# First weight pieces rounded and fetched later, and three more pairs turned by 32 x 32 squares

## The chip, the cores and the metric

The kernel runs on one core of a Trainium2 chip. The metric is device time in microseconds (us) of that core. The time before is the median of three runs, 1395.97 us (1393.84 to 1398.77).

## The reference

Attention with RMS-normalised q and k, 8 batches of 12 heads, 448 tokens, 64 dimensions; then two matrix products with `h - tanh(h)` between them on the 3584 x 768 result.

```python
q_n, k_n = rmsnorm(q, g_q), rmsnorm(k, g_k)          # x / sqrt(mean(x*x) + 1e-6) * g
scores = scale * matmul(q_n, k_n.transpose(0, 1, 3, 2))
scores = scores - max(scores)                        # over the last axis
attn = exp(scores)
attn = attn / (sum(attn) + 1e-9)
out = matmul(attn, v)                                # (8, 12, 448, 64)
x = out.transpose(0, 2, 1, 3).reshape(3584, 768)
h = x @ w_in                                         # 768 x 2048
g = h - tanh(h)
return g @ w_out                                     # 2048 x 768
```

w_in and w_out come as float64. The kernel takes them as pairs of 32-bit words and rounds them to float32 on the chip.

## The kernel before

**Pairs and slots.** The unit of attention is a pair of heads: 8 batches of six pairs (`NP`) are 48 pairs, counted from 0, so the 16th pair is pair 15. The program is a list of slots written out by hand; slot s finishes pair s, makes the scores of pair s+1, turns (transposes) q and k of pair s+2 and squares or normalises pair s+3. Slots -3 to 5 are `first_slot` (L943), 6 to 11 `early_slot` (L977), 12 to 47 `slot` (L1005). Instructions go to each engine's queue in the order in which this code makes them: PE (matmuls), ACT (exps, copies, squares), DVE, POOL, and SP, which issues nearly all DMAs.

**The MLP.** While attention of batch b+1 runs, a generator gives the matmuls of batch b's two products; `run(ns)` puts that many ns of them between the parts of a slot. In `first_slot` there is no MLP work yet. Later batches read their weights from a ring of six places in `w_f`, fetched five products ahead (`ring_load`, L379).

**Weights.** There are 32 pieces (`PIECES`) of 768 KB raw, 16 of w_in and 16 of w_out. `weight_load(n)` (L254) fetches one, as four DMAs for w_in. The first eight (`EARLY`) land in the memory that is `gT` later, which has four places (`NSTAGE`); the others in three buffers `w_raw`. Rounding has three steps: `round_weight_a` (two ACT instructions, L71 and L72), `round_weight_b` (three on DVE, L78 to L82) and `round_weight_c` (one on POOL, L90). `weight(to)` (L290) rounds up to `to` pieces: step a of piece n, steps b and c of piece n-1, and then it fetches on to piece n+3, as long as a place is free (`place_free`). The last lines of `first_slot(s)` call it with `8 * (s + 3) // 8`, that is one piece by the end of slot -2 and one more in each slot after. Piece 0 is fetched before all slots.

**q and k, two ways.** The plain way: `load` fetches q of a pair so that each of 112 partitions holds four neighbouring tokens, and k in blocks of 128; `squares` (ACT) and `norm` (DVE, POOL) give each token's factor, `norm_q` scales q, and `turn` (L416) transposes k and q with eight PE matmuls against the identity (L421, L425) and two ACT copies. k's factor goes into the exp as its scale (`rr`). The way by blocks: `load_blocks` (L439) fetches squares of 32 tokens by 32 dimensions in eight DMAs, `square_blocks` (ACT), `norm_blocks` (DVE and one POOL power), `scale_blocks` (DVE), and `turn_blocks` (two DVE transposes, one ACT scaling): no PE instruction. The exp then needs no scale. The tiles of this way live in a pool that is opened when the first batch's MLP has been written out (`late["blocks"]`), after slot 11.

Which way a pair goes, and in which order tokens lie, is set by one constant: `FIRST, NJ = 3, S // BL` (L434) and

```python
def by_blocks(s):
    return has(s) and steps[s][0] >= FIRST
```

so pairs from 18 on (batch 3) go by blocks. `store` (L822), which transposes and writes the result, undoes the plain way's order of tokens for batches below `FIRST`.

## Time and profile before

| what | us |
|---|---|
| median of three runs | 1395.97 |
| lowest, highest | 1393.84, 1398.77 |
| profiled execution, device time | 1397.86 |
| its span, first to last instruction | 1396.1 |
| DVE, ACT, POOL busy | 940.3, 507.9, 555.4 |
| DMA engines busy (queue of SP), share | 63.8% |
| q_nat loads, issue to landing, median | 4.5 |
| gT loads (weight pieces), issue to landing, median | 4.2 |
| qk_nat loads (blocks), issue to landing, median | 2.3 |

In the lines below, a timeline row gives start, duration, engine, line, operation, `output<-input`, shapes and how often, and in brackets how long the engine sat idle before it and what ended that. `SPq` rows are DMAs being issued. PE's matmul ends are modelled, so that a busy PE need not be PE at its peak. Each fp32 matmul counts twice in some rows of the timeline.

### The profile page before, as it was taken

What the parts mean: (1) busy time and instruction counts of PE and PEld (TensorE: products, weight loads), DVE (VectorE), ACT (ScalarE), POOL (GpSimd) and SP (SyncE); (2) the same over time, 40 slices, a digit from 0 to 9 for tenths busy, and PEclk for the clock granted to TensorE, in tenths of its full rate; (3) what the DMA queues carried; (4) which work ended last, traced back from release to release, by engine and by line L of the source; (5) the groups of instructions that cost most, each with busy time, mean ns of one, the idle gap of its engine ahead of it and who ended that gap; (6) DMA issues with size and microseconds to landing.
All of it is one profiled execution on the core that took longest, in us unless ns stands there. A gap on an engine that the chain in (4) does not pass through costs nothing.

```text
span 1396.1 us, 29929 instructions
## 1 busy us (share of the span) xinstructions
PE 1360.6 (97%) x11864; PEld 1133.3 (81%) x11864; DVE 940.3 (67%) x1530; ACT 507.9 (36%) x1153; POOL 555.4 (40%) x348
## 2 busy tenths in 40 slices
PE   6999899999999999999999999999999999999997
PEld 2468664478899898889889988988988998899997
DVE  3999888757756688567867668656885677632311
ACT  5866554234423433233332333224333243301100
POOL 4665555224432347224544245423462255402310
PEclk9999999999999999999999999999999999999999
DMA  7769788765556756666656666666556656366663
GB/s 177 175 189 245 244 253 214 207 198 166 158 142 192 182 163 182 170 155 193 181 148 176 195 156 184 184 156 176 171 166 176 172 179 192 100 189 183 192 192 89
DMA packets 355273, 250.01 MB, mean 179 GB/s; under 512 B 266484, under 2 KB 297396, under 8 KB 355124
## 3 DMA queue, kind: packets, MB, share of 16 engines
q1 hardware_dynamic: 355120, 248.00, 63.8%
q8 instruction: 96, 1.57, 0.5%
q14 instruction: 53, 0.43, 0.1%
q10 hardware_dynamic: 4, 0.00, 0.0%
HBM read 214.50 MB, written 33.42 MB: 178 GB/s over the span
## 4 chain that ended last, share of the span: by engine, by line
PE 87%; DVE 5%; DMA 3%; ACT 2%; SPq 1%; issue 1%; POOL 0%; DVEq 0%; ACTq 0%
PE mm L733 65%; PE sc L506 9%; PE sc L567 6%; PE mm L898 4%; PE sc L555 1%; DMA q_nat<-in_q_dram 1%; PE sc L605 1%; DMA w_raw<-in_moe_w_out_dram 1%; DMA w_f<-w_out 1%; DMA w_raw<-in_moe_w_in_dram 1%; DVE w_out L82 1%; PE mm L605 1%; DVE w_out L78 0%; DVE rs L631 0%; ACT p L512 0%
## 5 line engine op out<-in xcount | busy, mean ns | idle before, releaser
L733 PE MATMUL mm<-xT,w_f 128*128 128x224 f32 x1392 | 278.2, 354 | 1.4 <-DVE s L789 1.4
L733 PEld LDWEIGHTS mm<-xT,w_f 128*128 128x128 f32 x1392 | 261.3, 190 | 15.0 <-issue 10.2
L733 PEld LDWEIGHTS mm<-gT,w_f 128*128 128x128 f32 x1344 | 252.8, 190 | 12.8 <-issue 12.8
L733 PE MATMUL mm<-gT,w_f 128*128 128x224 f32 x1344 | 263.0, 354 | 0.0
L506 PE MATMUL sc<-qT,kT 64*32 64x448 f32 (+1 forms) x3072 | 219.1, 505 | 12.8 <-ACT p_last L512 9.4
L463 POOL TENSOR_TENSOR rr_mine<-rr_mine,neg_half 128x28 f32<-128x28 f32 x30 | 145.1, 4835 | 203.3 <-DVE rr_mine L462 203.3
L733 PE MATMUL mm<-tt,w_f 128*128 128x224 f32 x1044 | 208.7, 353 | 0.0
L733 PEld LDWEIGHTS mm<-tt,w_f 128*128 128x128 f32 x1044 | 197.0, 190 | 4.4 <-issue 4.4
L733 PE MATMUL mm<-tg,w_f 128*128 128x224 f32 x1008 | 197.7, 353 | 0.0
L770 POOL TENSOR_TENSOR gT<-s,th 128x448 f32<-128x448 f32 x96 | 118.6, 1245 | 188.1 <-ACT th L769 181.6
L733 PEld LDWEIGHTS mm<-tg,w_f 128*128 128x128 f32 x1008 | 190.6, 190 | 0.0
L506 PEld LDWEIGHTS sc<-qT,kT 64*32 64x32 f32 x3072 | 72.3, 107 | 84.3 <-issue 58.8
L671 DVE TENSOR_TENSOR xT<-xT,sc 128x448 f32<-128x448 f32 x35 | 21.7, 621 | 163.3 <-PE sc L506 118.5
L693 POOL TENSOR_TENSOR tt<-xT,tt 128x224 f32<-128x224 f32 x23 | 31.4, 1366 | 240.5 <-DVE xT L675 217.5
L650 ACT COPY sum_g<-sum 32x14 f32<-32x14 f32 x280 | 56.2, 201 | 180.8 <-DVE sum L642 175.0
L567 PE MATMUL sc<-p,v_nat 64*32 64x448 f32 x1120 | 110.5, 536 | 0.0
L769 ACT ACTIVATE th<-s 128x448 f32<-128x448 f32 x96 | 55.3, 576 | 114.4 <-DVE s L795 57.2
L135 POOL TENSOR_TENSOR rr<-rr,neg_half 112x8 f32<-112x8 f32 (+1 forms) x36 | 59.6, 1676 | 61.5 <-DVE rr L134 37.4
L512 ACT ACTIVATE p<-sc 128x448 f32<-128x448 f32 x120 | 65.2, 543 | 46.8 <-PE sc L506 34.5
L898 PE MATMUL mm<-gT,w_out 128*128 128x448 f32 x192 | 76.8, 556 | 0.3 <-POOL w_out L90 0.3
L898 PEld LDWEIGHTS mm<-gT,w_out 128*128 128x128 f32 x192 | 36.6, 195 | 39.3 <-issue 37.2
L567 PEld LDWEIGHTS sc<-p,v_nat 64*32 64x32 f32 x1120 | 40.6, 107 | 31.1 <-issue 31.1
(151 smaller groups left out, 1853.1 us busy)
## 6 DMA issues: line engine op xcount, KB each, us to landing
w_f<-w_in SPq DMA_DIRECT2D x196, 384.0 KB, 3.3
w_f<-w_out SPq DMA_DIRECT2D x147, 512.0 KB, 3.8
w_raw<-in_moe_w_out_dram SPq DMA_DIRECT2D x16, 768.0 KB, 5.0
out_dram<-th SPq DMA_DIRECT2D x192, 56.0 KB, 1.9
w_in<-w_out SPq DMA_DIRECT2D x21, 384.0 KB, 6.7
qk_nat<-in_q_dram SPq DMA_DIRECT2D x120, 56.0 KB, 2.3
qk_nat<-in_k_dram SPq DMA_DIRECT2D x120, 56.0 KB, 2.4
gT<-in_moe_w_in_dram SPq DMA_DIRECT2D x32, 192.0 KB, 4.2
```

The source lines that it names most:

```text
L135: nc.gpsimd.tensor_tensor(out=r, in0=r, in1=neg_half[:rows], op=ALU.pow)
L463: nc.gpsimd.tensor_tensor(out=mine, in0=mine, in1=neg_half[:, :1].to_broadcast([P, 2 * NJ]), op=ALU.pow)
L506: nc.tensor.matmul(tiles[h][i * BL : (i + 1) * BL, :n], lhsT=kT[r, c * P + at : c * P + at + BL], rhs=qT[r, first : first + n], start=True ...
L512: nc.scalar.activation(p[:, h, c if c < 2 else 0, :], tiles[h][:, :n], AF.Exp, scale=1.0 if rr is None else rr[:, 0, 2 * c + h : 2 * c + h ...
L567: nc.tensor.matmul(av[g][i * BL : (i + 1) * BL, :S], lhsT=v_nat[keys, h, c, m * BL : (m + 1) * BL], rhs=p[keys, h], start=first, stop=True ...
L605: nc.tensor.matmul(av[n][r : r + BL, :HS], lhsT=v_nat[:, h, c, m * BL : (m + 1) * BL], rhs=p[c][:, h, n * HS : (n + 1) * HS], start=False, ...
L650: nc.scalar.copy(out=acc[h * BL : (h + 1) * BL, g], in_=part[g * BL : (g + 1) * BL, h * NJ : (h + 1) * NJ])
L693: eng.tensor_tensor(out=t2, in0=x22, in1=t1, op=ALU.subtract)
L733: nc.tensor.matmul(bank[:, f * HS : (f + 1) * HS], lhsT=w[:, c * width + f, :], rhs=moving[p](c), start=(first and f == 0 and c == 0), sto ...
L769: nc.scalar.activation(th, h, AF.Tanh, bias=0.0, scale=1.0)
L770: eng.tensor_tensor(out=g[:, rows, cols], in0=h, in1=th, op=ALU.subtract)
L898: nc.tensor.matmul(bank[:, :S], lhsT=w_out_row(f, n // HC)[:, n % HC * P : (n % HC + 1) * P], rhs=g[:, f, :], start=(f == 0), stop=(f == C ...
```

## The change

1. `weight` no longer fetches itself but calls a new `load_weights(to)`; for pieces below 5 it fetches on to piece n+2 in place of n+3. At the end of slot -2, nothing is rounded: `load_weights(2)` fetches piece 1 alone. Piece 0 is rounded at the end of slot -1, together with piece 1.
2. `FIRST` goes from 3 to 2, and now sets the order of tokens alone (`in_order`): pairs from 12 on are fetched with rows in natural order, with new branches in `fetch` for q and k (q in two DMAs for one, all in pieces of 256 bytes). `store` takes plain columns from batch 2 on.
3. `by_blocks` asks for `s >= TURNED`, 2 * 6 + 3 = 15. Pairs 15, 16 and 17 go by blocks too. Pair 15's blocks are fetched near the end of slot 12; the others as before at the start of a slot.

On the engines' queues: PE loses 24 transposes; ACT has piece 0's two instructions 14 places later; on SP, the twelve weight DMAs of slot -2 become four and the four of slot -1 become eight; the fetching stays one piece behind the old order until slot 3, where the two are level again.

```diff
@@ fetch
     if name == "q":
+        if in_order:
+            for h in range(2):
+                nc.sync.dma_start(out=t[:, h], in_=pair[h].rearrange("(c p) d -> p c d", c=NCH))
+            return
...
     if name == "v":
         last = t[:, :, KF]
+    elif in_order:
+        last = t[:, KF]
     if in_order:
         for h in range(2):
-            nc.sync.dma_start(out=t[:, h, :KF], in_=pair[h, : KF * P].rearrange("(c p) d -> p c d", p=P))
+            to = t[:, h, :KF] if name == "v" else t[:, :KF, h]
+            nc.sync.dma_start(out=to, in_=pair[h, : KF * P].rearrange("(c p) d -> p c d", p=P))
@@ load
-                fetch(nc, name, t, src[b, 2 * hp : 2 * hp + 2], by_blocks(s))
+                fetch(nc, name, t, src[b, 2 * hp : 2 * hp + 2], in_order(s))
@@ weight
+    def load_weights(to):
+        while done[0] < min(to, PIECES) and place_free(done[0]):
+            weight_load(done[0])
+            done[0] += 1
...
-            while done[0] < min(n + 4, PIECES) and place_free(done[0]):
-                weight_load(done[0])
-                done[0] += 1
+            load_weights(n + (3 if n < EARLY - 3 else 4))
@@ order of tokens, blocks
-    FIRST, NJ = 3, S // BL
+    FIRST, NJ = 2, S // BL
+    TURNED = 2 * NP + 3
     def by_blocks(s):
+        return has(s) and s >= TURNED
+    def in_order(s):
         return has(s) and steps[s][0] >= FIRST
@@ first_slot
-        weight(EARLY * (s + 3) // (NP + 2))
+        if s == -2:
+            load_weights(2)
+        else:
+            weight(EARLY * (s + 3) // (NP + 2))
@@ early_slot
-        if has(s + 4):
+        if has(s + 4) and not by_blocks(s + 4):
             load(s + 4, "qk")
@@ slot
-        if by_blocks(s + 3):
+        if by_blocks(s + 3) and s + 3 > TURNED:
             load_blocks(s + 3)
...
+        if s + 3 == TURNED:
+            load_blocks(s + 3)
         if ahead:
             norm_q(s + 3)
```

## The prediction

> **What bounds the kernel now.** I read, in this order: the engines' busy shares, the chain of work that ended last, the timeline of the first 40 us, a table by stretches of the same time, and the times at which each slot's `p_last` exps start. All times are of the profiled execution: 1397.86 us, of which the span is 1396.1.

> ```profile
> PE 1360.6 (97%) x11864; PEld 1133.3 (81%) x11864; DVE 940.3 (67%) x1530; ACT 507.9 (36%) x1153; POOL 555.4 (40%) x348
> ...
> PE 87%; DVE 5%; DMA 3%; ACT 2%; SPq 1%; issue 1%; POOL 0%; DVEq 0%; ACTq 0%
> ```

> TensorE is the bound, and 87% of the last chain is its own work. So a saving is either PE work taken out, or one of the few places where PE is not last. The first 36 us are such a place:

> ```profile
> 10.00 3.24 PE L506 MATMUL sc<-qT,kT 64*32 64x448 f32 x32 [0.62 <-ACT qT L429]
> ...
> 15.19 0.89 ACT L71 ACTIVATE w_out<-gT 128x768 f32<-128x768 f32 x1 [3.98 <-DMA gT<-in_moe_w_in_dram]
> ...
> 16.11 6.39 SPq L265 DMA_DIRECT2D gT<-in_moe_w_in_dram  x12
> 16.75 2.19 ACT L512 ACTIVATE p<-sc,rr 128x448 f32<-128x448 f32 x4
> ...
> 23.25 0.31 SPq L99 DMA_DIRECT2D q_nat<-in_q_dram  x1
> ...
> 24.11 2.24 ACT L512 ACTIVATE p<-sc,rr 128x448 f32<-128x448 f32 x4
> ...
> 31.42 0.63 ACT L123 ACTIVATE n<-q_nat 112x512 f32<-112x512 f32 x1 [4.12 <-DMA q_nat<-in_q_dram]
> ...
> 36.05 2.21 ACT L512 ACTIVATE p<-sc,rr 128x448 f32<-128x448 f32 x4
> ```

> Pair 0's scores are done by 13.2, but ACT first waits 3.98 us for the first weight piece (L71) and starts the exps (L512) at 16.75. Then twelve weight DMAs (three pieces) go out in one block, the q load of pair 3 gets onto the queue only at 23.25, and ACT waits 4.12 us for it. Slot 0 therefore lasts from 24.11 to 36.05, 11.94 us; the next three, exp to exp, last 9.67, 9.51 and 9.47. Stretch by stretch, the columns being us, PE, PEld, DVE, ACT, POOL, PE clock, DMA share, GB/s:

> ```profile
> 10.00:17.00 7.00, 4.95 (x40) 2.10 (x40) 2.31 (x5) 2.91 (x5) 3.24 (x2) 1.00 0.92 219
> 17.00:24.00 7.00, 6.41 (x69) 1.97 (x70) 2.53 (x6) 7.00 (x14) 2.58 (x2) 0.76 0.98 217
> 24.00:36.00 12.00, 10.32 (x169) 4.86 (x170) 5.62 (x10) 7.71 (x15) 5.69 (x4) 1.00 0.90 199
> ```

> The transfers are saturated here (0.92 to 0.98 busy, about 217 GB/s), so the order on SP decides who waits. In the second part of the change the reader is to look at the slots' lengths:

> ```profile
> 319.51 0.79 ACT L512 ACTIVATE p_last<-sc,rr 128x224 f32<-128x224 f32 x2 [3.09 <-PE sc L506]
> ...
> 402.49 0.79 ACT L512 ACTIVATE p_last<-sc,rr 128x224 f32<-128x224 f32 x2 [8.45 <-PE sc L506]
> ...
> 429.30 0.60 ACT L512 ACTIVATE p_last<-sc 128x224 f32<-128x224 f32 x2 [5.03 <-PE sc L506]
> ...
> 456.11 0.61 ACT L512 ACTIVATE p_last<-sc 128x224 f32<-128x224 f32 x2 [5.02 <-PE sc L506]
> ```

> Slots 13, 14 and 15 take 82.98 us together; the slots after them, where q and k go by squares of 32, take 26.81 each.

> [...] exps with finished scores stand 3.98 us behind a rounding that waits for its data. [...] the trace has 0.76 in the stretch 17 to 24, after a PE wait of 2.5 us[...]. [...] a median packet of 1024 B takes 47 ns, 768 B 36, 256 B 18 and 128 B 13, that is 22, 21, 14 and 10 bytes per ns.

> **The change part by part.**

> *First weights.* Slot -2 no longer rounds piece 0 (L71, L72); both piece 0 and piece 1 are rounded at the end of slot -1, behind pair 0's exps. ACT in slot -1, from rows of the trace: chunk 0's scores are half of the 3.24 us, so ready at 11.6, and chunk 1's at 13.2; its exps end at 14.3; kT and qT of pair 1 (0.53 each) follow the transposes and end at 15.5; the squares of pair 2 wait for k, whose last piece lands at 16.8, and end at 17.4; `p_last` 0.7 and `p_full` 1.06 end at 19.2. Rounding piece 0 costs 1.65 (0.8 each), to 20.8. Rounding piece 1 must wait: its last DMA, whose place on SP is unchanged (issued at 17.69), lands at 22.2. It ends at 23.8, and slot 0's exps start then, 0.3 earlier than 24.11. So the wait at L71 is mostly turned into one for piece 1. The larger gain is in slot 0. Pieces 2 and 3 (eight DMAs, 0.86 us each on the saturated engines, 6.9 us) now stand behind pair 3's q and k, which land at about 24.4 instead of 31.3 and are wanted at 27. The 4.12 us wait is gone. What is late next is PE: the `p_last` scores get their banks at 25.0, last values and values take 3.0 to 3.6, the last scores start at 28.6 and let `p_full` start 1.1 later (as at 41.93 and 43.06), 29.7; plus 1.06 and 1.65 this gives slot 1's exps at 32.4 against 36.05: 3.65 earlier. If slot 0 takes the 9.5 of later slots instead, 33.3, or 2.75 earlier. I take 3.5, ends 2.5 and 4.2.

> Does the lag starve the rounding? Piece 2 lands after pair 3 and v of pair 1 at about 28.9, and is wanted at 30.8; piece 3 at 32.4, wanted at 40. From slot 3 (n = 5) the loads stand where they stood. DVE's and POOL's steps b and c keep their slots. From 36 us on nothing depends on absolute time: loads are released by buffers, roundings by due times counted in matmuls, so I expect the whole rest to shift by what slot 1 gained. The DMA engines are idle for 0.3 of 36 to 46 and 0.2 of 46 to 58, so the same bytes in 3.5 us less are carried.

> *Squares of 32 for pairs 15, 16, 17.* Out of PE: 3 turns of four k and four q transposes. The chain prices a turn at 0.44 + 0.39 = 0.83 us, so 2.5 us; the slots say 82.98 - 3 × 26.81 = 2.55. I take 2.5, ends 2.0 and 2.7, because the later slots already run with all the work that is added here. That is, per pair: on DVE one reduction 1.06, four copies 0.17, two small ones 0.37, the scaling 1.24, two transposes 1.27, together 4.6 us, for 2 × 0.68 + 2 × 0.17 + one `norm_q` of 0.6 to 2.7; on POOL one power of 4.78 for two of 1.62; on ACT 0.95 + 0.67 for 2.3 or so. DVE is busy 14 to 23 us in these slots of 27 to 28, POOL 10 to 12: PE hides it. Were that cover gone, the late kT would hold the next slot's first scores by the overrun alone. Pair 15's load goes from slot 11 to the end of slot 12, and its squaring from slot 12 to slot 13, some 13 us after the issue, with 2.3 us to landing: covered. SP gets eight DMAs (4.2 us) ahead of ring loads that are fetched five products ahead, each product 12 or more matmuls of 0.19 us: covered, as in all later slots.

> *Loads in order.* q and k of pairs 12 to 14 and v of pairs 12 to 17 go in pieces of 256 B: q 896 packets of 18 ns for 224 of 47, k's main part 768 of 18 for 256 of 36, over 16 engines 0.65 us more per pair, and one more issue of 0.6 us each on SP. They fall in slots 8 to 10, a slot ahead of use: nothing, at most 1.5 us if they hold up w_out pieces for which PE already waits there. Batch 2's stores read plain columns instead of strided ones: nothing.

> Sum: 3.5 + 2.5 = 6.0, so 1397.86 becomes 1391.9. The profiled execution lies 1.89 above the median of the three runs (1395.97, from 1393.84 to 1398.77); the same saving from the median gives 1390.0. A difference of 0.3%, 4.2 us, is about what a measurement of this kernel can tell from no change.

> **The rivals.** (B) *The start's gain is swallowed.* From 60 to 160 us DVE is 97% busy with roundings and combinations; if that stretch is paced by weights and not by when attention arrives, only 2.5 us remain: 1393.5. Against it: DVE is idle 1.9 of the 12 us from 46 to 58, so it carries no backlog into it, and the pieces come in by released buffers. (C) *Rounding starves.* ACT rounds in front of the next slot's exps; if piece 2 lands after 30.8 (my slack is 1.9 us) and the shorter lead keeps pieces 2 to 6 late, each by one piece's transfer of 3.45 us, five slots lose 17 us: 1407, slower. For it: transfers are saturated to 40 us. Against: one piece less is in flight than before. (D) *A later stall goes too.* At 170.91 PE waits 5.39 us for an exp behind a w_out piece, then runs the next stretch at clock 0.74; the changed phase may take away 6 us: 1384. The same phase could as well cost that; I count this in the range of the others.

> **How the numbers follow.** Forecast 0.60 at 1390.0 (its own range 1387.5 to 1392.5), B 0.22, C 0.09, D 0.09. The range 1385.5 to 1396.5 holds forecast and B whole with the unknown costs, leaving out C and D. Faster by over 0.3% means below 1391.8: 0.85 of the forecast and D, 0.60. Slower is C, 0.09. The rest, 0.31, is within 0.3%.

> **What would show it.** Right: the first exps at about 11.6; L123 of slot 0 no longer waiting for DMA; slot 1's exps near 32.4; slots 13 to 15 at 26.8 and 24 matmuls fewer on PE. Wrong: ACT waiting for `gT` in slots 0 to 3 (C); the first batch's MLP starting 3.5 us earlier but its end not (B); a new PE wait of microseconds between 160 and 290.

## The result, and the profile after

| | before | after |
|---|---|---|
| median of 20 runs, us | 1397.32 | 1393.93 |
| lowest, highest | 1393.37, 1399.12 | 1390.53, 1396.42 |
| profiled execution, its span | 1397.86, 1396.1 | 1394.93, 1393.0 |

The ratio is 0.9974, 95% interval 0.9968 to 0.9981: 3.6 us saved (interval 2.7 to 4.5) where 6.0 were forecast. The whole interval lies below 1, so the gain is real, though 3.6 us is less than the 0.3% (4.2 us) that one measurement of this kernel can tell from none. The forecast of 1390.0 lies 3.9 below the measured median: 2.6 of it because less was saved (3.4 between the medians), 1.35 because the kernel before took 1397.32 in these 20 runs and not the 1395.97 of the first three. L71 and the lines up to 90 keep their numbers; L512 became L527 (exps), L506 L521 (scores), L123 L130 (squares of q), L733 L748 (MLP), L789 L804 (a sum of the MLP on DVE).

The page of the changed kernel, busy time and the engines' shares of the chain that ended last:

```profile
PE 1358.7 (98%) x11840; PEld 1131.3 (81%) x11840; DVE 938.9 (67%) x1545; ACT 504.3 (36%) x1147; POOL 561.3 (40%) x345
...
PE 87%; DMA 4%; DVE 4%; ACT 1%; SPq 1%; issue 1%; POOL 0%; DVEq 0%; ACTq 0%
```

24 matmuls have gone (11864 to 11840), and PE still carries 87% of the chain. The timeline of ACT and PE in slot 0, after:

```profile
23.19 0.90 ACT L71 ACTIVATE w_out<-gT 128x768 f32<-128x768 f32 x1 [2.12 <-DMA gT<-in_moe_w_in_dram]
...
24.77 2.18 ACT L527 ACTIVATE p<-sc,rr 128x448 f32<-128x448 f32 x4
25.43 0.94 PE L521 MATMUL sc<-qT,kT 64*32 64x224 f32 x9 [2.82 <-ACT p L527]
27.76 0.66 ACT L130 ACTIVATE n<-q_nat 112x512 f32<-112x512 f32 x1
28.42 1.72 PE L620 MATMUL mm<-p,v_nat 128*32 128x224 f32 x16
...
33.06 3.04 PE L521 MATMUL sc<-qT,kT 64*32 64x448 f32 x48
34.43 1.16 ACT L527 ACTIVATE p_full<-sc,rr 128x448 f32<-128x448 f32 x2 [4.82 <-PE sc L521]
...
37.10 2.22 ACT L527 ACTIVATE p<-sc,rr 128x448 f32<-128x448 f32 x4
```

The wait of 4.12 us for q is gone: L130 at 27.76 has no bracket. But the last line, slot 1's exps, stands at 37.10, where before had 36.05: the start is later, not earlier. The lines are to be read from the last one upwards. The exps of `p_full` waited 4.82 us for their scores, which PE began at 33.06. In front of those on PE are the values (L620), of which a group of 16 took 1.72 us. Before them PE had waited 2.82 us for the exps, and these stood behind a rounding that waited 2.12 us for piece 1. The table by stretches, after (us, PE, PEld, DVE, ACT, POOL, PE clock, DMA share, GB/s), says why the values were slow:

```profile
17.00:24.00 7.00, 4.53 (x70) 2.24 (x70) 4.32 (x8) 4.82 (x9) 5.03 (x3) 1.00 0.98 216
24.00:36.00 12.00, 10.04 (x128) 3.86 (x128) 6.54 (x13) 7.18 (x15) 3.63 (x3) 0.72 0.94 209
```

Before, the low clock (0.76) lay in the stretch 17 to 24, where ACT was about to wait for q anyway. Now it lies in 24 to 36 (0.72), on the path. The trace's clock records give it as half speed for 6.8 us from 26.7. In the second part, the slots' `p_last` exps, first before (slots 14 and 15) and then after (slots 13 to 16):

```profile
347.16 0.79 ACT L512 ACTIVATE p_last<-sc,rr 128x224 f32<-128x224 f32 x2 [1.50 <-PE sc L506]
...
374.89 0.78 ACT L512 ACTIVATE p_last<-sc,rr 128x224 f32<-128x224 f32 x2 [1.64 <-PE sc L506]
```

```profile
318.42 0.79 ACT L527 ACTIVATE p_last<-sc,rr 128x224 f32<-128x224 f32 x2 [3.09 <-PE sc L521]
...
345.23 0.61 ACT L527 ACTIVATE p_last<-sc 128x224 f32<-128x224 f32 x2 [1.50 <-PE sc L521]
...
372.93 0.61 ACT L527 ACTIVATE p_last<-sc 128x224 f32<-128x224 f32 x2 [0.74 <-PE sc L521]
399.72 0.61 ACT L527 ACTIVATE p_last<-sc 128x224 f32<-128x224 f32 x2 [4.87 <-PE sc L521]
```

Slot 13 takes 26.81 and slot 15 26.79, but slot 14 takes 27.70, as long as before (27.73) although its turn is gone. The three save 82.98 - 81.30 = 1.68 us.

The 3.1 us of span between the two executions are thus made up: 0.1 lost by slot 7's exps (121.72 to 121.83), 1.2 gained from there to slot 12's `p_last` (290.93 to 289.84), 1.68 in slots 13 to 15, 0.3 after slot 18. The 1.2 is hardly the change's: the clock records have a half-clock stretch of 6.8 us at 240.0 before and one of 3.4 us at 241.8 after, and half of the difference, an estimate of what it cost, is 1.7.

### The profile page after: what moved, and what is told of

The parts are those of the page before. It is cut to its first block, busy times and chain, and to the rows that moved or that the text cites. A ratio compares the mean times of both kernels' runs of the same rounds, so it can differ in the third digit from the quotient of the medians.

```text
span 1393.0 us, 29913 instructions
## 1 busy us (share of the span) xinstructions
PE 1358.7 (98%) x11840; PEld 1131.3 (81%) x11840; DVE 938.9 (67%) x1545; ACT 504.3 (36%) x1147; POOL 561.3 (40%) x345
## 4 chain that ended last, share of the span: by engine, by line
PE 87%; DMA 4%; DVE 4%; ACT 1%; SPq 1%; issue 1%; POOL 0%; DVEq 0%; ACTq 0%
PE mm L748 66%; PE sc L521 8%; PE sc L582 6%; PE mm L913 4%; PE sc L570 1%; DMA w_f<-w_out 1%; DMA gT<-in_moe_w_in_dram 1%; PE sc L620 1%; DMA q_nat<-in_q_dram 1%; DMA w_raw<-in_moe_w_out_dram 1%; PE sc L641 1%; SPq L125 1%; DMA k_nat<-in_k_dram 0%; PE mm L620 0%; ACT p L527 0%
## 5 line engine op out<-in xcount | busy, mean ns | idle before, releaser
L748 PE MATMUL mm<-xT,w_f 128*128 128x224 f32 x1392 | 278.5, 355 | 1.7 <-DVE s L804 1.7
L748 PEld LDWEIGHTS mm<-xT,w_f 128*128 128x128 f32 x1392 | 261.3, 190 | 16.0 <-issue 10.2
L748 PEld LDWEIGHTS mm<-gT,w_f 128*128 128x128 f32 x1344 | 252.8, 191 | 12.8 <-issue 12.8
L748 PE MATMUL mm<-gT,w_f 128*128 128x224 f32 x1344 | 263.0, 354 | 0.0
L478 POOL TENSOR_TENSOR rr_mine<-rr_mine,neg_half 128x28 f32<-128x28 f32 x33 | 159.7, 4840 | 218.2 <-DVE rr_mine L477 218.2
L521 PE MATMUL sc<-qT,kT 64*32 64x448 f32 (+1 forms) x3072 | 216.4, 501 | 12.1 <-ACT p_last L527 8.3
L748 PE MATMUL mm<-tt,w_f 128*128 128x224 f32 x1044 | 208.8, 353 | 0.0
L748 PEld LDWEIGHTS mm<-tt,w_f 128*128 128x128 f32 x1044 | 197.0, 191 | 4.4 <-issue 4.4
L748 PE MATMUL mm<-tg,w_f 128*128 128x224 f32 x1008 | 197.5, 353 | 0.0
L748 PEld LDWEIGHTS mm<-tg,w_f 128*128 128x128 f32 x1008 | 190.7, 191 | 0.0
L521 PEld LDWEIGHTS sc<-qT,kT 64*32 64x32 f32 x3072 | 72.2, 107 | 82.3 <-issue 59.6
L527 ACT ACTIVATE p<-sc 128x448 f32<-128x448 f32 x132 | 71.7, 543 | 51.7 <-PE sc L521 39.1
L142 POOL TENSOR_TENSOR rr<-rr,neg_half 112x8 f32<-112x8 f32 (+1 forms) x30 | 49.7, 1680 | 38.1 <-DVE rr L141 38.0
```

The source lines that it names most:

```text
L142: nc.gpsimd.tensor_tensor(out=r, in0=r, in1=neg_half[:rows], op=ALU.pow)
L478: nc.gpsimd.tensor_tensor(out=mine, in0=mine, in1=neg_half[:, :1].to_broadcast([P, 2 * NJ]), op=ALU.pow)
L521: nc.tensor.matmul(tiles[h][i * BL : (i + 1) * BL, :n], lhsT=kT[r, c * P + at : c * P + at + BL], rhs=qT[r, first : first + n], start=True ...
L527: nc.scalar.activation(p[:, h, c if c < 2 else 0, :], tiles[h][:, :n], AF.Exp, scale=1.0 if rr is None else rr[:, 0, 2 * c + h : 2 * c + h ...
L748: nc.tensor.matmul(bank[:, f * HS : (f + 1) * HS], lhsT=w[:, c * width + f, :], rhs=moving[p](c), start=(first and f == 0 and c == 0), sto ...
```

## Experiments

Each ratio is against the kernel before, run beside it; the changed kernel's is 0.9974 (0.9968 to 0.9981).

**The first part alone.** The code before, with `load_weights` and slot -2 of the change.

> The kernel before with the first part of the change alone (piece 1 alone fetched in slot -2, both first pieces rounded in slot -1, fetching one piece less ahead). Theory 1, the prediction's: 3.5 us faster than before, a ratio of about 0.9975, slot 1's exps near 32.4. Theory 2: the wait for piece 0 became one for piece 1, in which PE also fell to half clock, and the stretch of 55 to 99 us is paced by DVE; so slot 1's exps come near 37, about 1 us later than the 36.05 of before, the MLP of the first batch starts within 0.3 us of 99.6, and the time is that of before within 1 us (0.9993 to 1.0007).

Ratio 0.9990 (0.9982 to 0.9999), about 1.4 us saved. Slot 0 looked as in the changed kernel: half clock from 26.7, slot 1's exps at 37.35, slot 7's at 122.16. The profiled execution agrees with theory 2. On the mean, theory 1's 0.9975 lies outside the interval; theory 2's 0.9993 to 1.0007 overlaps its upper end, but leaves no room for 1.4 us.

**The second part alone.**

```diff
-            load_weights(n + (3 if n < EARLY - 3 else 4))
+            load_weights(n + 4)
@@ first_slot
-        if s == -2:
-            load_weights(2)
-        else:
-            weight(EARLY * (s + 3) // (NP + 2))
+        weight(EARLY * (s + 3) // (NP + 2))
```

> The changed kernel with the first weights handled as before, so the order of loads and the squares of 32 for pairs 15, 16 and 17 alone. Theory 1, the prediction's: 2.5 us faster than before (0.9982), slots 13 to 15 at 26.8 each. Theory 2: slot 14 keeps its 27.7, since every sixth slot (20, 26, 32, 38, 44 of before too) takes 27.6 for a wait on DVE that the turn had covered in slot 14; 1.7 us faster (0.9988). If the first part is worth nothing, this kernel must be nearly as fast as the changed one (0.9974); if it reaches only 0.9988, about 2 us of the changed kernel's gain come from the first part after all.

Ratio 0.9983 (0.9975 to 0.9991), about 2.4 us; slots 13 to 15 took 26.81, 27.70 and 26.79. The interval holds 1.7 and 2.5 both. The two parts add up to 3.8, the whole change's 3.6 within error.

**Piece 1 rounded in slot 0.**

```diff
-            weight(EARLY * (s + 3) // (NP + 2))
+            weight(1 if s == -1 else EARLY * (s + 3) // (NP + 2))
...
             load(s + 4, "qk")
+        if s == 0:
+            weight(2)
         if s > -3:
             squares(s + 3)
```

> The changed kernel, but slot -1 rounds piece 0 alone and piece 1 is rounded in slot 0, behind the two turned copies and ahead of the squares; so slot 0's exps no longer stand behind a rounding that waits for its data. Theory 1 (the fault lies in that one wait, and absolute time counts for nothing afterwards): slot 0's exps near 21, slot 1's near 33, 4 us before the changed kernel's, and the whole about 3 us faster than the changed kernel (0.995 of before). Theory 2 (DVE paces the first batch's weights): slot 1's exps come as early, but the first batch's MLP starts at 99 to 99.8 as in both kernels and the time stays that of the changed kernel within 1 us (0.997). A third outcome: PE drops to half clock in slot 0 here too, and slot 1's exps stay at 35 to 37.

Ratio 0.9956 (0.9944 to 0.9969). The timeline of ACT in slots 0 and 1:

```profile
21.42 2.23 ACT L527 ACTIVATE p<-sc,rr 128x448 f32<-128x448 f32 x4
...
24.41 1.02 ACT L71 ACTIVATE w_out<-gT 128x768 f32<-128x768 f32 x1
...
31.79 0.97 ACT L71 ACTIVATE w_out<-gT 128x768 f32<-128x768 f32 x1 [2.36 <-DMA gT<-in_moe_w_in_dram]
...
33.49 2.20 ACT L527 ACTIVATE p<-sc,rr 128x448 f32<-128x448 f32 x4
```

Slot 0's exps come 3.35 us earlier than in the changed kernel, slot 1's 3.6. Slot 7's come at 119.98, 1.85 earlier: what was lost between is a half clock of 3.4 us at 37.1. So an early start is carried on to the MLP, which speaks for theory 1; piece 2, at 31.79, is the next to be late.

**The same with the longer lead.** As above, and `load_weights(n + 4)`.

> The staggered rounding (piece 1 in slot 0), and pieces fetched to n+3 as before the change. With the shorter lead ACT waited 2.36 us at 31.79 for piece 2, and slot 1's exps came at 33.49. Theory (that wait is the price of the shorter lead): no wait for gT longer than 1 us in slot 0 or 1, slot 1's exps at 31 to 32, about 2 us less than the staggered kernel (0.994 of before against 0.9956). Rival (transfers are saturated, so an earlier issue only delays q and k): ACT waits for q or k instead and the time is that of the staggered kernel.

Ratio 0.9963 (0.9949 to 0.9977), no gain: ACT still waits 2.09 us for piece 2 at 31.32, where under 1 us was expected. The lead is not the reason; which transfer should give way wasn't tried.

**Folding of the sums later in every sixth slot.** Folding is a transpose and a reduction of the exps' sums on DVE (L655 and L657).

```diff
-        if folded:
+        if folded and s % NP != 2:
             fold(s + 1)
         run(gap / 2)
+        if folded and s % NP == 2:
+            fold(s + 1)
```

> The changed kernel with the folding of the sums (a transpose and a reduction on DVE, 1.11 and 1.09 us) made one quarter of a gap of MLP work later in every sixth slot (14, 20, 26, 32, 38, 44), so that the MLP's sum at L804 no longer stands behind it on DVE. Theory 2 (slot 14's turn was cover for a wait of PE for that sum): slot 14 and its five companions fall from 27.6 or 27.7 to about 26.9, together 4.5 us, and the time falls to about 0.9942 of before. Rival: the slots are long because of POOL's power, the work of the hidden layer's last set or the clock; then they stay at 27.6 and the time at 0.9974.

Ratio 0.9970 (0.9957 to 0.9982), and slot 14 stays at 27.70. First its place in the changed kernel, from the timelines of DVE and PE:

```profile
362.11 1.11 DVE L655 STREAM_TRANSPOSE sum_T<-rows 128x896 f32<-128x896 f32 x1
363.25 1.09 DVE L657 TENSOR_REDUCE sum<-sum_T 128x28 f32<-128x896 f32 x1
364.25 0.61 DVE L804 TENSOR_TENSOR s<-mm,s 128x448 f32<-128x448 f32 x1
364.84 2.01 DVE L485 TENSOR_TENSOR qk_n<-qk_nat,rr_mine 128x896 f32<-128x896 f32 x1
366.78 0.61 DVE L806 TENSOR_TENSOR s<-mm,s 128x448 f32<-128x448 f32 x1
...
364.92 5.06 PE L748 MATMUL mm<-xT,w_f 128*128 128x224 f32 x24 [0.32 <-DVE s L804]
```

PE waits for L804, which reads the `mm` tile that the next product writes, and L804 stands behind the folding. The bracket shows only a part of the loss: from 362.17, where the product ahead begins, PE takes 10.01 us to the next slot's scores at 372.18; in the kernel with folding and scaling later, below, it takes 9.17. The other 0.5 us lies within the rows, whose ends are modelled. Then with the folding later:

```profile
357.68 0.62 DVE L804 TENSOR_TENSOR s<-mm,s 128x448 f32<-128x448 f32 x1
...
360.41 2.02 DVE L485 TENSOR_TENSOR qk_n<-qk_nat,rr_mine 128x896 f32<-128x896 f32 x1
362.36 0.61 DVE L806 TENSOR_TENSOR s<-mm,s 128x448 f32<-128x448 f32 x1
...
363.02 2.54 PE L748 MATMUL mm<-xT,w_f 128*128 128x224 f32 x12 [0.57 <-DVE s L806]
```

L804 now comes early, and PE waits for the next sum, L806, behind the scaling: a wait that takes the place of the one removed.

This run's trace told more by its start, whose code is that of the changed kernel. Slot 0, ACT and PE:

```profile
22.31 0.92 ACT L71 ACTIVATE w_out<-gT 128x768 f32<-128x768 f32 x1 [0.90 <-DMA gT<-in_moe_w_in_dram]
...
23.90 2.20 ACT L527 ACTIVATE p<-sc,rr 128x448 f32<-128x448 f32 x4
24.59 0.94 PE L521 MATMUL sc<-qT,kT 64*32 64x224 f32 x9 [1.69 <-ACT p L527]
...
26.68 0.58 PE L570 MATMUL mm<-p_last,v_nat 64*32 64x224 f32 x8 [0.59 <-ACT kT L434]
27.20 0.96 PE L620 MATMUL mm<-p,v_nat 128*32 128x224 f32 x16
...
29.61 2.80 PE L521 MATMUL sc<-qT,kT 64*32 64x448 f32 x48
30.74 1.16 ACT L527 ACTIVATE p_full<-sc,rr 128x448 f32<-128x448 f32 x2 [1.96 <-PE sc L521]
...
33.41 2.22 ACT L527 ACTIVATE p<-sc,rr 128x448 f32<-128x448 f32 x4
```

No half clock before 72.5, and slot 1's exps at 33.41, slot 7's at 118.22: 3.5 us earlier than before, the size of the forecast. From this came theory 3.

**Folding and scaling later.** The scaling goes one quarter of a gap later too, in the same slots.

```diff
+        if folded and jam:
+            fold(s + 1)
-        if blocks:
+        if blocks and not jam:
             scale_blocks(s + 2)
...
         run(gap / 2)
+        if blocks and jam:
+            scale_blocks(s + 2)
         if blocks:
             turn_blocks(s + 2, 0)
```

> The changed kernel with the folding and the scaling of the squares both made later in every sixth slot (14, 20, 26 and so on). With the folding alone moved, the sum at L804 came 3 us earlier, but the next sum, L806, then stood behind the scaling (L485, 2.02 us, which waits for POOL's power), PE waited 0.57 us for it and the slot stayed at 27.70. Theory (DVE's order holds PE in these slots): 26.9 in all six, together 4.5 us, 0.9942 of before. Rival (DVE has too much work there whatever the order; from 345 to 368 it has no gap): a third wait appears, 27.5 to 27.7 as before, 0.997.

Ratio 0.9946 (0.9933 to 0.9960). The `p_last` exps of slots 14 and 15, and PE between them:

```profile
345.28 0.61 ACT L527 ACTIVATE p_last<-sc 128x224 f32<-128x224 f32 x2 [1.50 <-PE sc L521]
...
362.22 6.97 PE L748 MATMUL mm<-xT,w_f 128*128 128x224 f32 x36
...
372.14 0.60 ACT L527 ACTIVATE p_last<-sc 128x224 f32<-128x224 f32 x2 [0.31 <-PE sc L521]
```

PE no longer waits in slot 14, which takes 26.86; its five companions take 26.76 to 26.91. This profiled execution had the half clock in slot 0 as well (slot 1's exps at 36.67), so the gain isn't the start's.

**PE kept busy in slot 0, eight matmuls.** Here a kernel does work that nobody reads.

```diff
+        if s == 0:
+            for _ in range(8):
+                nc.tensor.matmul(av[0][:, :S], lhsT=ident, rhs=turned[1][1], start=True, stop=True)
         if has(s + 1):
             scores(s + 1, KF)
```

> The changed kernel with eight more matmuls of 128x448 on PE in slot 0, ahead of the p_last scores, into a bank that is written anew afterwards; nobody reads them, about 0.37 us each, 3 us in all, in the time in which PE waited 2.82 us for the exps. Theory 3 (the start's gain is lost whenever PE falls to half clock in slot 0, and is there whenever it doesn't: slot 1's exps at 37.1 and 37.35 in two executions with the fall, at 33.41 in one without it): no half clock between 20 and 40 us, slot 1's exps between 33.4 and 34.3, slot 7's near 118.3 instead of 121.8, and the median 1.5 to 3 us below the changed kernel's, a ratio of 0.995 to 0.9965. Rival (it is piece 1's late landing, 23.1 against 22.2, that decides, or the eight matmuls only delay PE): slot 1's exps at 35 to 37 and a ratio of 0.997 or more.

Ratio 0.9979 (0.9968 to 0.9990). PE and ACT in slot 0:

```profile
22.61 6.28 PE L978 MATMUL mm<-kT,ident 128*128 128x448 f32 x16
...
28.82 0.61 PE L521 MATMUL sc<-qT,kT 64*32 64x224 f32 x16
...
35.98 1.15 ACT L527 ACTIVATE p<-sc,rr 128x448 f32<-128x448 f32 x2
```

The half clock is gone, but the price was mis-read: eight took 6.28 us, and the ratio came out as the rival had it. The timeline counts each twice (x16 for eight), so a 128x448 costs 0.78 (6.28 by eight) and not the estimated 0.37 (twice the 0.19 of a counted 128x224, 6.97 by 36), and the filling was longer than the wait.

**Three matmuls.**

> The changed kernel with three more matmuls of 128x448 on PE in slot 0, that nobody reads, where eight were put before. The eight took 6.28 us (0.77 each, twice what was reckoned), 3 us more than PE's wait, so they held up the p_last scores until 28.82; there was no half clock, and slot 1's exps came at 35.98. Three take 2.3 us, within the wait. Theory 3 (the start's gain is lost where PE falls to half clock in slot 0): no half clock from 20 to 40 us, slot 1's exps at 33.4 to 34.4, slot 7's at 118.2 to 119.2, and a ratio of 0.9955 to 0.9968. Rival (slot 1 is late for another reason, or later stretches swallow what the start gains): slot 1 at 35.5 to 37, or slot 7 at 121 to 122 in spite of an early slot 1, and 0.997 to 0.998.

Ratio 0.9963 (0.9949 to 0.9976). PE and ACT:

```profile
22.65 2.52 PE L978 MATMUL mm<-kT,ident 128*128 128x448 f32 x6
23.63 0.93 ACT L71 ACTIVATE w_out<-gT 128x768 f32<-128x768 f32 x1 [2.37 <-DMA k_nat<-in_k_dram]
25.23 2.20 ACT L527 ACTIVATE p<-sc,rr 128x448 f32<-128x448 f32 x4
25.92 0.94 PE L521 MATMUL sc<-qT,kT 64*32 64x224 f32 x9 [0.75 <-ACT p L527]
...
34.74 2.20 ACT L527 ACTIVATE p<-sc,rr 128x448 f32<-128x448 f32 x4
```

Here ACT waited until 23.63. (The bracket names a load of k; L71 reads the weight piece alone, so this is taken as the wait for piece 1.) Only in the first part alone was it as late, so slot 1's exps miss the expected window by 0.34 and slot 7's, at 119.45, by 0.25; the ratio is within. But slot 0 lasts 9.51 and not 12.33. The rival that piece 1's late landing decides is out: in the first part alone the same rounding started at 23.64, with the half clock, and slot 1's exps came 2.6 us later than here. With folding and scaling later, and with the work first, it started early, at 22.46 and 22.21, and the half clock came all the same. All executions in which both first pieces are rounded in slot -1, side by side:

| kernel | PE's wait ahead of the p_last scores | half clock in slot 0 | slot 0, us | slot 1's exps | slot 7's exps |
|---|---|---|---|---|---|
| changed | 2.82 | from 26.7, 6.8 us | 12.33 | 37.10 | 121.83 |
| first part alone | 2.99 | from 26.7, 6.8 us | 12.15 | 37.35 | 122.16 |
| folding and scaling later | 1.81 | from 26.5, 6.8 us | 12.62 | 36.67 | 121.42 |
| work first (below) | 1.70 | from 25.6, 6.8 us | 12.26 | 36.07 | 120.80 |
| both changes of order (below) | 2.52 | from 26.95, 6.8 us | 12.41 | 37.25 | 121.99 |
| folding later | 1.69 | none | 9.51 | 33.41 | 118.22 |
| eight matmuls | none | none | 12.01 | 35.98 | 120.70 |
| three matmuls | 0.75 | none | 9.51 | 34.74 | 119.45 |
| both, with matmuls (below) | none | none | 9.50 | 33.29 | 117.98 |

**MLP work ahead of the p_full scores in slots 6 to 11.**

```diff
         divide(s, values(s, av))
+        run(gap / 2)
         if has(s + 1):
             scores(s + 1, 2)
-        for work, n in ((add, 1), (add_last, 1), (norm, 3), (norm_q, 3)):
+        run(gap / 2)
+        for work, n in ((add, 1), (add_last, 1)):
+            if has(s + n):
+                work(s + n)
+        for work, n in ((norm, 3), (norm_q, 3)):
             run(gap / 2)
```

> The changed kernel with one quarter of slots 6 to 11's MLP work put ahead of the p_full scores, for whose bank PE waits 5.05 us at 170.72 and 1.93 us at 240.87, behind an exp that ACT does after a rounding. Theory (PE stands idle there though it has MLP work, and the half clock of 6.8 and 3.4 us afterwards follows from the idle time): both waits shrink to under 1 us, no half clock between 160 and 260 us, slot 12's p_last 5 to 12 us before the changed kernel's 289.84, and a ratio of 0.989 to 0.994. Rival (the w_out pieces pace this stretch, so PE waits for its weights instead): slot 12 within 2 us of 289.84, 0.996 to 0.9975.

Ratio 0.9919 (0.9905 to 0.9932): PE's wait at 170 falls from 5.05 to 2.06 us (under 1 was expected), the one at 241 is gone, no half clock lies between 81 and 1380 us, and slot 12's `p_last` comes at 279.87.

**Both changes of order, then with matmuls in slots 0 and 5.** The second kernel adds three matmuls as above in slot 0, and three into the bank of the q transposes in slot 5; nobody reads them.

```diff
-            turn(s + 2, mm_bank(), sc_bank())
+            tk, tq = mm_bank(), sc_bank()
+            for _ in range(3 if s == 5 else 0):
+                nc.tensor.matmul(tq[:, :S], lhsT=ident, rhs=turned[6][1], start=True, stop=True)
+            turn(s + 2, tk, tq)
```

> The changed kernel with the MLP work ahead of the p_full scores in slots 6 to 11 (0.9919 alone) and with folding and scaling later in every sixth slot (0.9946 alone, against 0.9974 of the changed kernel). The two lie in different stretches, so their gains should add: 0.9919 - 0.0028 = 0.989, about 1382 us where the kernel before takes 1397, and slots 14, 20 and so on at 26.9. If the second were only luck of the clock in the first batch, it would add nothing, 0.992.

> The kernel with both changes of order, and three matmuls of 128x448 that nobody reads in slot 0 and three in slot 5, where PE waits 2.42 us for a reciprocal at 76.54 and a half clock of 3.4 us follows. Theory 3: no half clock after 20 us but at the end, so 1.5 to 3 us off for slot 0 and up to 1.7 us off for slot 5, 0.986 to 0.988. Rival (the matmuls hold up as much as they save, or DVE's pace from 60 to 90 us hides the half clock of slot 5): 0.989 as without them.

Ratios 0.9887 (0.9872 to 0.9902), median 1381.2, and 0.9865 (0.9850 to 0.9880), median 1378.2. The gains add, and no execution of the one overlaps the other's (1380.3 to 1381.6, and 1377.2 to 1379.1). In the second one's trace, ACT in slots 0 and 1:

```profile
23.79 2.19 ACT L527 ACTIVATE p<-sc,rr 128x448 f32<-128x448 f32 x4
...
33.29 1.14 ACT L527 ACTIVATE p<-sc,rr 128x448 f32<-128x448 f32 x2
```

The half clocks of slots 0 and 5 are gone. One of 3.4 us at 167.2, which wasn't expected, is left, and the one at the end.

**The last one without the first part of the change**, and without the matmuls of slot 0.

> The last kernel with both changes of order, with the first weights handled as before the change and without the three matmuls of slot 0 (those of slot 5 stay). Theory 3 (the first part is worth some 3 us wherever PE keeps its clock in slot 0): slot 0 takes 11.3 to 11.9 us as before, for ACT's wait for q; slot 1's exps at 35.9 to 36.2 against 33.29, slot 7's near 120.5 against 117.98, and about 2.5 to 3 us more than the kernel with the first part: 1380.7 to 1381.2, a ratio near 0.9885. Rival (the first part is worth the 1 to 1.4 us that it showed alone, whatever the clock): 0.9872 to 0.9875.

Ratio 0.9892 (0.9875 to 0.9910), median 1381.53, 3.3 us more than with the first part (the kernel before, beside each, took 1396.82 and 1396.63). Slot 1's exps came at 36.47 and slot 7's at 122.11, later than the 120.5 expected. The intervals of the two ratios overlap between 0.9875 and 0.988, but the profiled executions differ by 3.2 us at slot 1 and 4.1 at slot 7.

## Why the prediction was right and wrong

**Slot -1: right.** The first exps came at 12.12 (11.6 forecast), piece 1 was waited for until 23.19 (22.2), slot 0's exps came at 24.77 (23.8; 24.11 before). In the trace with the folding later the last two are 22.31 and 23.90. The landing moves by a microsecond or so between executions: in the nine traces that round both first pieces in slot -1, the rounding of piece 1 starts between 22.14 and 23.64.

**The wait for q: right.** It is gone, and neither ACT nor DVE waits for a weight piece in slots 0 to 3. Rival C fell.

**Slot 0: here it failed.** The step was "last values and values take 3.0 to 3.6 ... this gives slot 1's exps at 32.4". It gave PE in slot 0 the pace of later slots. But the change takes away what PE did in the wait for slot 0's exps (the scores of slot -1 are over sooner, those exps are not), so PE idles for 1.7 to 3 us. In five of the six traces with this start and no added matmuls a half clock of 6.8 us follows, on the path to slot 1; in the three with added matmuls none does. The values of slot 0 took 4.64 us (28.42 to 33.06) where they take 2.41 at full clock (27.20 to 29.61 in the trace with the folding later), and the scores around them slowed as well. With the half clock the term of 3.65 us at slot 1 measured -1.05 in the profiled execution; without it, 2.64. The prediction had the means: it quoted 0.76 after a wait of 2.5 us before, and didn't ask where the same would lie afterwards.

The step was also too short at full clock. In the trace with the folding later PE began the `p_last` scores at 24.59 and the last scores at 29.61, 5.0 us where the sum had 3.6: in slot 0 PE follows ACT, and the last values waited 0.59 us for kT, which ACT copies behind the exps. Slot 0 took 9.51 us, the 9.5 that the prediction kept as its other reading (2.75 earlier). That 3.5 was met at slot 7 with the folding later is in part luck: 0.9 of it came in slots 1 to 6, half of that in slot 4 (9.95 us before, 9.48 here), where PE's wait of 0.55 us for DVE is gone. The sum had nothing for it. In the medians of the last pair the first part, with the matmuls of slot 0, is worth 3.3.

Averaged over executions the first part alone gave 1.4 (0.1 to 2.5). That this mean is a mixture of executions with and without the half clock is an inference from the traces above. The mean clock that is on record for every execution bears it out: in the changed kernel the twelve at 0.991 took 1394.7 us on the mean, the five at 0.992 1392.4 and the three at 0.993 1390.9; of the kernel before, in the executions beside the experiments, seventeen at 0.991 took 1397.2 and fifteen at 0.993 1395.7. These means don't say where the half clock lay, so how often slot 0 has it stays open.

**"From 36 us on nothing depends on absolute time": right for a gain.** What the folding-later and three-matmul traces gained by slot 1 (2.64 and 1.31) is there at slot 7, with 0.9 more. Rival B, the swallowed gain, had the result's size (1393.5) by luck: what swallowed the gain was the half clock before slot 1. A loss is taken up: the changed kernel was 1.05 late at slot 1 and 0.11 late at slot 7: slots 1 to 4 were 0.6 shorter, slot 5 0.4 longer, and PE's wait of 0.75 us for a sum on DVE, at 99.60 before, is no longer there. (The prediction had DVE 97% busy from 60 to 160 us; the trace before gives 94.65 of the 100 us.)

**Squares of 32: mechanism right, size too large.** Slots 13 and 15 gained 0.84 and 0.81, a turn each. Slot 14 gained 0.03. The step that failed was "the slots after them ... take 26.81 each": every sixth does not. Slots 20, 26, 32, 38 and 44 take 27.56 to 27.66 in the kernel before too, and slot 14 is at the same phase of the batch. It took 27.73 with the turn, and has the wait without it: the DVE jam of this phase takes back what the turn gave. The run with folding and scaling both later shows this, since all six slots fall to 26.8 or 26.9 together; with the folding alone later none did. What brought the wait can be estimated from the rows of slot 14 before:

```profile
364.94 6.97 PE L733 MATMUL mm<-xT,w_f 128*128 128x224 f32 x36
365.36 0.61 DVE L789 TENSOR_TENSOR s<-mm,s 128x448 f32<-128x448 f32 x1
```

Counted from the slot's `p_last` exps (347.16 before, 345.23 after), DVE ended this sum at 18.81 us before and ends it at 19.63 after, with the blocks' reduction and copies ahead of it. PE, whose product of 12 matmuls takes 2.27 us here, wants it at 20.05 before and at 19.21 after. So the later sum would have been in time for a PE that still had the turn, and the earlier sum for one that had not: by this estimate the wait takes both, the turn gone and the blocks' work on DVE. The prediction had put that work at nothing ("PE hides it"), from DVE's busy time in the whole slot.

1.68 for 2.5 is what the trace says, and slot 14 takes 27.69 to 27.71 in all eight traces with the squares and without the scaling moved. The run of the second part alone, with 1.3 to 3.5, can't decide between 1.7 and 2.5.

**Loads in order:** no loss seen. PE's waits at 170 and 241 were 5.05 and 1.93 us after, 5.39 and 2.50 before. Rival D, that one of them would go, didn't happen by the change; it did with the work ahead of the scores.

So the forecast missed by two terms: the start, 3.5 for a mean of 1.4, and the squares, 2.5 for 1.7 in the traces (2.4 in the mean of the second part alone).

## What to carry to other kernels

Ask of every stretch in which PE waits, several short waits included, not only what it costs but which matmuls run in the 7 us after it: the half clocks here lasted 3.4 or 6.8 us. Moving such a wait from in front of another stall to the path can take back a gain, as here at slot 1's exps, 37.10 for 36.05. Work put into it, useful if there is any, can save both the wait and the half clock, as long as it is no longer than the wait: three matmuls took 2.52 us and slot 0 then 9.51, eight took 6.28 and slot 0 then 12.01. Before a slot is priced by its neighbours, compare it with the slot one period later. And when PE's wait for another engine goes, look at the next instruction in that engine's queue that PE needs: it may wait behind the same crowd, as L806 did behind the scaling (0.57 us).

## What the runs showed of the hardware

The length of one wait didn't decide whether the clock fell. In slot 0 a wait of 1.70 us came with a fall in one execution (work first), and one of 1.69 in another (folding later) with none. In the staggered kernel with the longer lead the clock fell at 36.2 behind waits of 0.53 and 0.59 us: 16 matmuls of the values (L620) took 1.72 us from 36.35, where they take 0.96 at full clock in the trace with the folding later.

PE's busy share tells more in the two traces. In the 3.41 us ahead of each of the eight falls PE was busy for 0.00 to 1.55 us (0.00 to 0.46). In every other step of the grid at full clock, from 12 to 1370 us, it was busy for at least 1.84 us (0.54), and no fall followed. In other executions the share decides no better than the wait. By the timelines of PE it was 0.67 ahead of the fall at 36.2 (staggered, with the longer lead), 0.50 ahead of the one at 25.6 (work first), and 0.50 in the 3.41 us up to 24.7 (folding later, 14 steps of 3.41 ahead of its first fall at 72.5), where none followed. What makes the difference, the kind of matmuls or something else, stays open.

Falls at one place lasted 3.4 or 6.8 us: at some 240 us, 6.8 behind a wait of 2.50 before and 3.4 behind one of 1.93 after. At half speed 3.4 us more is up to 1.7 us of run-to-run difference at one place, an estimate from these two. The fall in slot 0 cost 2.6 to 3.1 us (12.15 to 12.62 against 9.51).
